# Turning the tokens of ten chunks with 32 by 32 block transposes on VectorE and a trip through DRAM, in place of TensorE transposes

## The chip, the core and the metric

The kernel runs on one core of a Trainium2 chip. The time is device time in microseconds (us) of one execution, the median of several runs. The engines are named as in the profile: PE is TensorE (PEld its weight loads), DVE is VectorE, ACT is ScalarE, POOL is GpSimd, SP is SyncE, which issues nearly all DMAs here.

## What is computed

Three layers follow each other, for batch 2, 768 tokens and 512 channels, all in float32. The part that the change touches is the middle one: each element of x is multiplied by the cosine and the sine of an angle, and the two products are mixed over the tokens.

```python
def _attn_ref(q, k, v):                      # 8 heads of 64: retention
    for t in range(S):
        state = gamma * state + outer(k[:, :, t], v[:, :, t])
        y[:, :, t] = scale * (q[:, :, t] @ state)

def _moe_ref(x, w_theta, w_tok_r, w_tok_i, w_ch):
    theta = x @ w_theta
    zr, zi = x * np.cos(theta), x * np.sin(theta)
    y = np.einsum('ts,bsd->btd', w_tok_r, zr) + np.einsum('ts,bsd->btd', w_tok_i, zi)
    u = x + y
    return u + np.maximum(u @ w_ch, 0.0)

def _moe2_ref(x, w_in, g_ln, w_sg, b_sg, w_out):
    h = gelu(x @ w_in); u, v = h[..., :512], h[..., 512:]
    v_s = np.einsum('ts,bsd->btd', w_sg, layernorm(v) * g_ln) + b_sg[None, :, None]
    return x + (u * v_s) @ w_out
```

## The kernel before

The 2 x 768 tokens are cut into twelve chunks of 128 tokens, 0 to 5 of the first batch and 6 to 11 of the second. A float32 product is made of three TensorE products of a high and a low part (`terms3`), so nearly every operand is split: ACT writes the high part (`split_hi`, L334), DVE the low part by a subtraction (`split_lo`, L340).

For each chunk, `retention` (L475) loads q, k and v in two halves of 512 KB (L460), forms scores (eight matmuls of 64 rows), a mask on DVE (L506), a faded v (ACT L529 or DVE L524), the outer products for the state, and `attend`. DVE then writes the chunk of x, L625, with the channels on the partitions and the tokens along the row (`x_chunk`), into the buffers `xa` and `xb`. `theta` (L647) multiplies it by the weights of the angle, in two halves of six matmuls of 512 columns, which gives angles with the tokens on the partitions; ACT and DVE make cosine and sine of them in one buffer `z` of 1024 words per partition. To be multiplied, x is needed with tokens on the partitions as well: `turn` (L717) has TensorE transpose four 128 by 128 blocks into a PSUM bank `tp`, and `times` (L725) is one DVE instruction of 1024 words that multiplies cosine and sine by it. z is split, and `mix_main` and `mix_rest` (L751, L778) mix it over tokens with weights that arrive as 1 MB loads (`weight`, L381: DMA, ACT L406, DVE L416 and L426, split). After them come the channel layer, the two up projections with gelu, the norm, the gate and the output products, none of which the change touches in what they compute.

An operation is an entry of a list of some 970. A table of numbers, `ORDER`, says in which order the planner (`Plan.schedule`) places them; it works out modelled start times with costs per engine, gives out buffers (`RAWS` raw loads, `PAIRS` buffers of 1024 words, `ONES` of 512) and sorts by start. Each engine then works through its own instructions in that order, and so does SP with the DMAs: a DMA that waits holds up those behind it. A gap of PE that the planner sees in the first microseconds is filled with idle matmuls on the identity (`keep_warm`).

Of the kernel before, what the change touches and what calls it, by code (L numbers as in the profile page):

```python
# [10 lines left out]
F32 = mybir.dt.float32  # L11
# [7 lines left out]
P = 128  # L19
# [17 lines left out]
N_WP = 19  # L37

RAWS, PAIRS, ONES = 2, 36, 7


class Buf:
# [21 lines left out]
class Plan:  # L64
# [105 lines left out]


ORDER = [
# [50 lines left out]
]  # L223


# [1 line left out]
def retention_spectral_gmlp(  # L227
# [10 lines left out]
):  # L238
    nc = tc.nc
    const = ctx.enter_context(tc.tile_pool(name="const", bufs=1))  # L240
    psum = ctx.enter_context(tc.tile_pool(name="psum", bufs=1, space=bass.MemoryType.PSUM))
    ctx.enter_context(tc.manual_schedule())
    V, A, G = nc.vector, nc.scalar, nc.gpsimd
# [19 lines left out]
    def bank():  # L263
        return Buf("psum")
# [33 lines left out]
    def x_chunk(i):  # L298
        b, c = divmod(i, NCH)
        if c < TA // P:  # L300
            return xa[b][:, :, c * P : (c + 1) * P]
        return xb[:, :, b, c * P - TA : (c + 1) * P - TA]
# [13 lines left out]
    def pe(dur, fn, **k):  # L316
        return plan.op("PE", dur, fn, **k)
# [5 lines left out]
    def dve(words, fn, ps=False, fast=False, **k):  # L323
        dur = 0.15 + words * (0.52e-3 if fast else 1.042e-3)
        return plan.op("DVE", dur, fn, port=not ps, **k)
# [149 lines left out]
    def retention(i):  # L475
# [168 lines left out]
            lambda: n4(h, F32R), lambda: n4(l, F32R), lambda: x_chunk(i), 512, t + 6, [*keys, h], [l]  # L644
        )

    def theta(i):  # L647
        b, c = divmod(i, NCH)
        t = T(i) + C['LT']
# [61 lines left out]
            w=[r],  # L711
            prio=t + 5.2,
        )
        tp = bank()
        keys = [("x", b, c, d) for d in range(NP)]

        def turn():  # L717
            for p in range(NP):
                nc.tensor.transpose(  # L719
                    out=ap(tp)[:, p * P : (p + 1) * P], in_=x_chunk(i)[:, p], identity=ident  # L720
                )

        pe(0.35, turn, form="turn", r=keys, w=[tp], prio=t + 5.3)

        def times():  # L725
            z2 = ap(z).rearrange("p (n t) -> p n t", n=2)
            V.tensor_tensor(  # L727
                out=z2, in0=ap(tp)[:, None, :].to_broadcast([P, 2, 512]), in1=z2, op=ALU.mult
            )

        dve(1024, times, ps=True, r=[tp], w=[co, r, z], prio=t + 6)
        split_hi(lambda: ap(zh, F32R), lambda: ap(z), 1024, t + 7, [z], w=[zh])
        split_lo(
            lambda: ap(zh, F32R), lambda: ap(zl, F32R), lambda: ap(z), 1024, t + 8, [z, zh], [zl]
        )
        zhl[i] = zh, zl

# [534 lines left out]
        weight(W_MAIN + s, T(s) + C['LW'])  # L1272
    for i in range(N):
        b, s = divmod(i, NCH)
        retention(i)
        theta(i)
        mix_main(b, s, T(i) + C['LM'])
        if i == NCH - 1:
            for k in range(NCH // 2):
                weight(W_REST + k, T(NCH) + C['LRW'] + 8 * k)  # L1280
        if s == NCH - 1:
            for k in range(NCH):
                mix_rest(b, k, T(i) + C['LR'] + (5 * k if b == 0 else 0.3 * k))
# [158 lines left out]
```

## Time and profile before

| | us |
|---|---|
| median of 3 runs (366.65 to 367.08) | 366.71 |
| the profiled execution | 367.32 |
| its span, first to last instruction | 365.6 |
| PE busy | 361.2 (99%) |
| DVE busy | 290.6 (79%) |
| ACT busy | 186.5 (51%) |
| POOL busy | 12.4 (3%) |

The span is what the trace shows; 1.72 us of the profiled execution lie around it. Busy times of engines overlap each other. A row of the timeline gives the start and the length of one merged run of instructions; the ends of matmuls are modelled, so for PE the distance between two starts is the better measure.

### The profile page before, as it was taken

To read this page: it belongs to the slowest core of one execution; us is meant where nothing else is said; L and a number is where in the kernel's file an instruction comes from. 1 tells how busy PE (TensorE), PEld (TensorE's weight loads), DVE (VectorE), ACT (ScalarE), POOL (GpSimd) and SP (SyncE) were. 2 spreads that over 40 slices of the span, in tenths; PEclk is the share of its full clock that TensorE was granted. 3 is DMA by queue.
4 is the path that set the end of the run, shared out by engine and by line. 5 is a ranking of instruction groups with operands and counts; after the bars stand their busy time and mean duration, and the time that the engine had idled before them with its cause. 6 is when DMAs were issued, how large, how long until landed. Compare 5 with 4: busy or idle time off the path is not lost.

```text
span 365.6 us, 5779 instructions
## 1 busy us (share of the span) xinstructions
PE 361.2 (99%) x2350; PEld 310.4 (85%) x2350; DVE 290.6 (79%) x456; ACT 186.5 (51%) x314; POOL 12.4 (3%) x18
## 2 busy tenths in 40 slices
PE   8999999999999999999999999999999999999996
PEld 7888888888999888888998888888888889988885
DVE  2788988987476978645688797989998996998894
ACT  3477979465363195611733434665687451252400
POOL 1021011000000220000000000000000000000000
PEclk9999999999999999999999999999999999999999
DMA  7999730174973411005042000001000000000034
GB/s 304 413 414 415 275 117 0 16 272 143 335 247 125 174 59 57 29 1 231 1 144 87 2 0 0 2 0 59 0 2 1 0 2 1 2 0 0 30 143 172
DMA packets 10346, 39.08 MB, mean 107 GB/s; under 512 B 1360, under 2 KB 2384, under 8 KB 7888
## 3 DMA queue, kind: packets, MB, share of 16 engines
q1 hardware_dynamic: 10176, 38.67, 28.3%
q8 instruction: 18, 0.29, 0.3%
q10 hardware_dynamic: 144, 0.05, 0.1%
q14 instruction: 8, 0.07, 0.1%
HBM read 35.57 MB, written 3.15 MB: 106 GB/s over the span
## 4 chain that ended last, share of the span: by engine, by line
PE 99%; DVE 0%; issue 0%
PE banks L314 97%; PE banks L719 1%; DVE b L1251 0%; DVE state L272 0%; DVE halfpi L276 0%
## 5 line engine op out<-in xcount | busy, mean ns | idle before, releaser
L314 PE MATMUL banks<-b,b 128*128 128x512 f32 (+2 forms) x1764 | 325.3, 351 | 0.0
L314 PEld LDWEIGHTS banks<-b,b 128*128 128x128 f32 (+1 forms) x1764 | 273.8, 183 | 45.6 <-issue 1.5
L334 ACT ACTIVATE b<-b 128x512 fp32r<-128x512 f32 (+1 forms) x83 | 62.6, 786 | 51.9 <-DVE b L1098 17.0
L340 DVE TENSOR_TENSOR b<-b,b 128x512 fp32r<-128x512 f32 (+1 forms) x83 | 70.2, 870 | 14.5 <-PE banks L314 8.9
L334 ACT ACTIVATE b<-xa 128x512 fp32r<-128x512 f32 (+1 forms) x26 | 17.0, 663 | 21.3 <-DVE xa L770 12.8
L406 ACT ACTIVATE b<-b 128x1024 f32<-128x1024 f32 x16 | 18.4, 1153 | 11.0 <-DMA b<-wts 11.0
L340 DVE TENSOR_TENSOR b<-xa,b 128x512 fp32r<-128x512 f32 (+1 forms) x26 | 18.7, 728 | 4.9 <-ACT b L334 4.9
L314 PE MATMUL banks<-b 64*128 64x128 f32 (+1 forms) x352 | 20.1, 262 | 0.0
L426 DVE SCALAR_TENSOR_TENSOR b<-b 128x1024 int32<-128x1024 int32 x16 | 19.5, 1220 | 0.5 <-ACT b L406 0.3
L314 PEld LDWEIGHTS banks<-b 64*128 64x128 f32 (+1 forms) x352 | 18.0, 171 | 1.9 <-issue 1.1
L506 DVE TENSOR_TENSOR b<-banks,causal 128x512 f32<-128x512 f32 x24 | 15.9, 685 | 4.5 <-PE banks L314 4.4
L334 ACT ACTIVATE b<-xb 128x512 fp32r<-128x512 f32 (+1 forms) x13 | 8.4, 669 | 18.9 <-DVE xb L806 6.3
L878 ACT ACTIVATE b<-b 128x512 f32<-128x512 f32 x24 | 14.8, 627 | 5.4 <-DVE b L868 5.4
L727 DVE TENSOR_TENSOR b<-banks,b 128x1024 f32<-128x1024 f32 x12 | 14.7, 1221 | 3.6 <-ACT b L710 1.4
L529 ACT ACTIVATE b<-b,dec 128x64 f32<-128x64 f32 x56 | 14.1, 334 | 5.4 <-DMA b<-qkv 5.4
L416 DVE TENSOR_SCALAR b<-b 128x1024 int32<-128x1024 int32 x16 | 10.9, 689 | 5.1 <-DMA b<-wts 5.1
L684 DVE SCALAR_TENSOR_TENSOR b<-banks,b 128x512 f32<-128x512 f32 x12 | 8.3, 689 | 7.9 <-PE banks L314 4.8
L675 ACT ACTIVATE b<-banks 128x512 int32<-128x512 f32 x12 | 7.1, 590 | 14.3 <-PE banks L314 14.3
L969 ACT ACTIVATE b<-b,rstd 128x512 f32<-128x512 f32 x12 | 9.6, 808 | 8.5 <-DVE rstd L958 8.5
L884 DVE SCALAR_TENSOR_TENSOR b<-b,banks 128x512 f32<-128x512 f32 x18 | 12.2, 680 | 1.7 <-ACT b L878 1.3
L868 DVE SCALAR_TENSOR_TENSOR b<-b,banks 128x512 f32<-128x512 f32 x18 | 11.9, 679 | 1.0 <-ACT b L860 0.9
L860 ACT ACTIVATE b<-banks 128x512 f32<-128x512 f32 x18 | 10.4, 593 | 4.5 <-PE banks L314 3.7
(74 smaller groups left out, 220.6 us busy)
## 6 DMA issues: line engine op xcount, KB each, us to landing
b<-wts SPq DMA_DIRECT2D x16, 1024.0 KB, 4.9
b<-qkv SPq DMA_DIRECT2D x24, 512.0 KB, 10.8
out<-b SPq DMA_DIRECT2D x11, 256.0 KB, 2.2
b<-wsg SPq DMA_DIRECT2D x9, 256.0 KB, 6.0
xa<-wts SPq DMA_DIRECT2D x2, 1024.0 KB, 11.7
xb<-wts SPq DMA_DIRECT2D x1, 1024.0 KB, 9.3
brow<-bvec SPq DMA_DIRECT2D x1, 384.0 KB, 5.8
dq<-qdecays SPq DMA_DIRECT2D x1, 256.0 KB, 6.3
```

The source lines that it names most:

```text
L314: nc.tensor.matmul(out=o, lhsT=l, rhs=r, start=start, stop=stop, skip_group_check=more)
L334: act(words, lambda: A.activation(out=hi(), in_=src(), func=AF.Copy), prio=prio, r=r, **k)
L340: lambda: E.tensor_tensor(out=lo(), in0=src(), in1=hi().bitcast(F32), op=ALU.subtract),
L406: lambda: A.activation(out=words(1).bitcast(F32), in_=words(1).bitcast(F32), func=AF.Prelu, scale=REBIAS, alpha=SIGN_UP,),
L416: lambda: V.tensor_scalar(out=words(0), in0=words(0), scalar1=29, scalar2=None, op0=ALU.logical_shift_right),
L426: lambda: V.scalar_tensor_tensor(out=words(0), in0=words(1), scalar=3, in1=words(0), op0=ALU.logical_shift_left, op1=ALU.bitwise_or,),
L506: V.tensor_tensor(out=ap(at[i])[:, h * 512 + lo : h * 512 + hi].rearrange("p (n t) -> p n t", n=n), in0=ap(sc[h])[:, lo:hi].rearrange("p ( ...
L529: A.activation(out=v, in_=v, func=AF.Copy, scale=dk[:, h : h + 1])
L727: V.tensor_tensor(out=z2, in0=ap(tp)[:, None, :].to_broadcast([P, 2, 512]), in1=z2, op=ALU.mult)
L868: lambda: V.scalar_tensor_tensor(out=ap(s), in0=ap(s), scalar=1.0 / GA, in1=ap(t), op0=ALU.add, op1=ALU.mult),
L878: lambda: A.activation(out=ap(s), in_=ap(s), func=AF.Tanh, scale=GA * GC),
L884: lambda: V.scalar_tensor_tensor(out=ap(o), in0=ap(s), scalar=1.0, in1=ap(t), op0=ALU.add, op1=ALU.mult),
```

## The change

Chunks 0 and 1 keep their `turn` on TensorE (`TURNED`). For the other ten, `by_token` takes the chunks in pairs (2 and 3, 4 and 5, 6 and 7, 8 and 9, 10 and 11). DVE transposes each chunk of x in blocks of 32 by 32 (`V.transpose`, 512 words per partition) into half of a buffer `tt`; SP writes `tt`, 512 KB, to a scratch tensor in DRAM; four DMAs of 128 KB read it back, each into 32 partitions, in runs of 256 words, so that the blocks land where a whole transpose would have put them. `times` becomes two DVE instructions of 512 words per chunk, which read the turned x from SBUF instead of a PSUM bank. The retention of a pair is listed before the angles of its first chunk, and the whole `ORDER` is another one. The counts of all other instructions stay, but for one `keep_warm` matmul less.

```diff
+TURNED = (0, 1)
...
 ORDER = [
-    48, 50, 49, 78, 77, 51, 105, 106, 0, 52, 161, 133, 55, 54, 56, 53, 189, 82, 57, 58, 134, 79, 6,
...
+    48, 50, 62, 49, 63, 105, 51, 106, 0, 52, 168, 118, 64, 53, 119, 55, 54, 56, 6, 67, 58, 57, 66,
...
+    dram = ctx.enter_context(tc.tile_pool(name="dram", bufs=1, space=bass.MemoryType.DRAM))
...
+    turned = {}
+
+    def by_token(i, t):
+
+        if i - i % 2 in turned:
+            return turned[i - i % 2]
+        tt, xt = Buf("pair"), Buf("pair")
+        turned[i - i % 2] = xt
+        for e in range(2):
+
+            def blocks(e=e):
+                V.transpose(
+                    out=ap(tt).rearrange("p (c e d k) -> p e d c k", c=4, e=2, d=NP)[:, e],
+                    in_=x_chunk(i + e).rearrange("p d (c k) -> p d c k", c=4),
+                )
+
+            b, c = divmod(i + e, NCH)
+            dve(
+                512, blocks, r=[("x", b, c, d) for d in range(NP)], w=[(tt, e)], prio=t + 4,
+            )
+        scr = dram.tile([P, 1024], F32, name=f"scr{i}")
+        dma(
+            512, lambda: nc.sync.dma_start(out=scr, in_=ap(tt)), r=[(tt, 0), (tt, 1)],
+            w=[("scr", i)], prio=t + 5,
+        )
+        for c in range(4):
+
+            def move(c=c):
+                nc.sync.dma_start(
+                    out=ap(xt)[32 * c : 32 * c + 32].rearrange("j (a q) -> j a q", a=4),
+                    in_=scr.rearrange("(a j) (c q) -> c j a q", a=4, c=4)[c],
+                )
+
+            dma(128, move, r=[("scr", i)], w=[(xt, c)], prio=t + 5)
+        return xt
...
+        if i in TURNED:
+            tp = bank()
...
+            dve(1024, times, ps=True, r=[tp], w=[co, r, z], prio=t + 6)
+        else:
+            xt = by_token(i, t)
+
+            def times(half):
+                v = ap(half).rearrange("p (d a k) -> p d a k", d=NP, a=4)
+                x = ap(xt).rearrange("p (a e d k) -> p e d a k", a=4, e=2, d=NP)[:, i % 2]
+                V.tensor_tensor(out=v, in0=x, in1=v, op=ALU.mult)
+
+            for half in (co, r):
+                dve(
+                    512, named(times, half), r=[(xt, a) for a in range(4)], w=[half, (z, half.k)],
+                    prio=t + 6,
+                )
...
-        retention(i)
+        if s % 2 == 0:
+            retention(i)
+            retention(i + 1)
         theta(i)
```

Three places where the order differs. The first is PE from its first matmul on. Before (`b_95`, `b_102`, `b_105`: q and k of chunks 0, 1, 2; `b_98`, `b_100`, `b_107`: their v; `ident` alone: keep-warm):

```order
L314 MATMUL banks<-state_64 128x128 x6
L314 MATMUL banks<-ident 128x128 x3
L314 MATMUL banks<-b_95 128x128 x8
L314 MATMUL banks<-ident 128x128 x2
L314 MATMUL banks<-b_98 64x64 x8
L314 MATMUL banks<-ident 128x128 x2
L314 MATMUL banks<-b_126,b_98 64x128 x8
L314 MATMUL banks<-b_102 128x128 x8
L314 MATMUL banks<-b_100 64x64 x8
```

After (`b_102`, `b_105`, `b_111`: q and k of chunks 0, 1, 2; `b_107`, `b_109`, `b_114`: their v):

```order
L319 MATMUL banks<-state_66 128x128 x6
L319 MATMUL banks<-ident 128x128 x3
L319 MATMUL banks<-b_102 128x128 x8
L319 MATMUL banks<-b_105 128x128 x8
L319 MATMUL banks<-ident 128x128 x3
L319 MATMUL banks<-b_107 64x64 x8
L319 MATMUL banks<-b_140,b_107 64x128 x8
L319 MATMUL banks<-b_111 128x128 x8
L319 MATMUL banks<-b_109 64x64 x8
L319 MATMUL banks<-b_105,state_67 64x128 x8
L319 MATMUL banks<-b_176,b_109 64x128 x8
L319 MATMUL banks<-b_114 64x64 x8
```

The scores of chunk 1 moved ahead of the first outer product, and the two gaps with two idle matmuls each became one gap with three.

The second place is SP's queue of DMAs after the first loads. Before (`xa`: the weights of the third mixing step; `b` from `wts`: later weights; `qkv`: later chunks):

```order
L395 DMA xa_87<-wts 128x2048
L460 DMA b_440<-qkv 128x1024
L395 DMA b_527<-wts 128x2048
L395 DMA b_628<-wts 128x2048
L395 DMA b_812<-wts 128x2048
L460 DMA b_820<-qkv 128x1024
```

After (`scr_91` and `scr_92`: the scratch of chunks 2 and 3, and of 4 and 5; `b_584`, `b_588`: chunk 9; `b_580`, `b_725`: the turned x of the two pairs):

```order
L400 DMA xa_89<-wts 128x2048
L674 DMA scr_91<-b_403 128x1024
L680 DMA b_580<-scr_91 32x4x256
L465 DMA b_584<-qkv 128x1024
L465 DMA b_588<-qkv 128x1024
L680 DMA b_580<-scr_91 32x4x256 x2
L400 DMA b_605<-wts 128x2048
L680 DMA b_580<-scr_91 32x4x256
L400 DMA b_675<-wts 128x2048
L674 DMA scr_92<-b_501 128x1024
L680 DMA b_725<-scr_92 32x4x256 x4
L400 DMA b_781<-wts 128x2048
```

The write and the four reads of a pair stand between loads of weights and of later chunks, and the last read of the first pair stands behind a 1 MB load.

The third place is DVE's queue where the first turned chunk is multiplied. Before (`L727`: `times` of chunk 1, from a PSUM bank):

```order
L340 TENSOR_TENSOR b_598<-b_367,b_586 128x1024
L570 TENSOR_TENSOR grown<-banks,state_65 128x256
L524 TENSOR_TENSOR b_379<-b_379,dec 128x2x256
L727 TENSOR_TENSOR b_475<-banks,b_475 128x1024
L340 TENSOR_TENSOR b_644<-b_463,b_632 128x1024
```

After (`L782`: `times` of chunk 2, from the turned x `b_580`; `L663`: the block transpose of chunk 5; the last row: the low part of z of chunk 2):

```order
L782 TENSOR_TENSOR b_614<-b_580,b_614 128x512
L663 STREAM_TRANSPOSE b_501<-xb 128x4x4x32
L431 SCALAR_TENSOR_TENSOR xa_89<-xa_89 128x1024
L529 TENSOR_TENSOR b_391<-b_391,dec 128x2x256
L782 TENSOR_TENSOR b_614<-b_580,b_614 128x512
L345 TENSOR_TENSOR b_715<-xa_89,b_706 128x1024
L511 TENSOR_TENSOR b_728<-banks,causal 128x512
L345 TENSOR_TENSOR b_731<-b_614,b_717 128x1024
```

One multiplication became two, with a block transpose and a weight's conversion between them, and they now wait for DMAs in place of PE.

## Rows read from the trace of the kernel before

**Rows 1.** The page, part 1: busy us, share of the span and instructions by engine.
```profile
PE 361.2 (99%) x2350; PEld 310.4 (85%) x2350; DVE 290.6 (79%) x456; ACT 186.5 (51%) x314; POOL 12.4 (3%) x18
```

**Rows 2.** The page, part 4: the chain that ended last, by engine and by line.
```profile
PE 99%; DVE 0%; issue 0%
PE banks L314 97%; PE banks L719 1%; DVE b L1251 0%; DVE state L272 0%; DVE halfpi L276 0%
```

**Rows 3.** Waits of PE: who for whom, us in total, times, longest.
```profile
PE banks L314 <- DVE halfpi L276: 1.2, 1, 1.2
```

**Rows 4.** Timeline of PE around turns (L719): start, length, line, operation, count.
```profile
54.24 0.60 PE L719 MATMUL banks<-ident,xa 128*128 128x128 f32 x4
54.59 1.63 PE L314 MATMUL banks<-b,b 128*128 128x512 f32 x6
56.06 0.60 PE L719 MATMUL banks<-ident,xb 128*128 128x128 f32 x4
56.41 8.44 PE L314 MATMUL banks<-b,b 128*128 128x512 f32 x36
64.69 0.60 PE L719 MATMUL banks<-ident,xa 128*128 128x128 f32 x4
...
133.72 16.59 PE L314 MATMUL banks<-b,b 128*128 128x512 f32 x72
150.15 0.60 PE L719 MATMUL banks<-ident,xb 128*128 128x128 f32 x4
```

**Rows 5.** Timeline of PE between retention matmuls and groups of 512 columns.
```profile
37.31 7.10 PE L314 MATMUL banks<-b,b 128*128 128x512 f32 x30
...
44.34 1.09 PE L314 MATMUL banks<-b,state 64*64 64x128 f32 x16
```

**Rows 6.** Timeline of PE at the start, to the first angles at 21.75.
```profile
5.37 2.08 PE L314 MATMUL banks<-b 64*128 64x128 f32 x16
...
7.38 0.71 PE L314 MATMUL banks<-ident 128*128 128x128 f32 x4
...
8.02 0.69 PE L314 MATMUL banks<-b 128*64 128x64 f32 x16
...
21.75 3.04 PE L314 MATMUL banks<-b,b 128*128 128x512 f32 x12
```

**Rows 7.** Timeline of ACT: the faded v of a chunk.
```profile
11.68 2.00 ACT L529 ACTIVATE b<-b,dec 128x64 f32<-128x64 f32 x8
```

**Rows 8.** DVE groups by form: busy us, mean ns of one, idle before.
```profile
L340 DVE TENSOR_TENSOR b<-b,b 128x512 fp32r<-128x512 f32 x55 | 36.1, 686 | 3.4 <-ACT b L334 3.2
L340 DVE TENSOR_TENSOR b<-b,b 128x1024 fp32r<-128x1024 f32 x28 | 34.3, 1233 | 11.1 <-PE banks L314 8.9 <-ACT b L334 2.1
...
L727 DVE TENSOR_TENSOR b<-banks,b 128x1024 f32<-128x1024 f32 x12 | 14.7, 1221 | 3.6 <-ACT b L710 1.4 <-ACT b L702 1.4 <-PE banks L719 0.8
...
L570 DVE TENSOR_TENSOR grown<-banks,state 128x256 f32<-128x256 f32 x8 | 3.3, 416 | 0.9 <-PE banks L314 0.9
```

**Rows 9.** Timeline of DVE: three instructions in a row, from start to start.
```profile
48.87 0.69 DVE L524 TENSOR_TENSOR b<-b,dec 128x512 f32<-128x512 f32 x1
49.47 1.23 DVE L727 TENSOR_TENSOR b<-banks,b 128x1024 f32<-128x1024 f32 x1
50.60 1.22 DVE L340 TENSOR_TENSOR b<-b,b 128x1024 fp32r<-128x1024 f32 x1
```

**Rows 10.** Stretches: us, busy PE, PEld, DVE, ACT, POOL, PEclk, DMA share, GB/s.
```profile
27.40:36.60 9.20, 9.20 (x106) 7.79 (x106) 7.92 (x12) 7.07 (x17) 1.70 (x2) 1.00 1.03 414
36.60:45.70 9.10, 9.10 (x66) 7.34 (x66) 8.32 (x12) 9.10 (x24) 0.00 (x0) 1.00 0.72 275
...
64.00:73.10 9.10, 9.10 (x45) 7.55 (x44) 8.32 (x10) 3.91 (x5) 0.00 (x0) 1.00 0.12 16
...
250.00:300.00 50.00, 50.00 (x228) 41.66 (x227) 45.34 (x114) 33.46 (x58) 0.00 (x0) 1.00 0.00 1
```

**Rows 11.** DMA issues: count, KB each, median us from issue to landing.
```profile
out<-b SPq DMA_DIRECT2D x2, 128.0 KB, 1.7
```

More of the change, by code (lines that the diff above doesn't have):

```diff
@@ L713, in theta, with turn, times @@
         )
[L714 to L720, printed above, removed]
-                )
[L723 to L732, printed above, removed]
+        if i in TURNED:
+            tp = bank()
+            def turn():
+                for p in range(NP):
+                    nc.tensor.transpose(
+                        out=ap(tp)[:, p * P : (p + 1) * P], in_=x_chunk(i)[:, p], identity=ident
+                    )
+            pe(
+                0.35, turn, form="turn", r=[("x", b, c, d) for d in range(NP)], w=[tp],
+                prio=t + 5.3,
+            )
+            def times():
+                z2 = ap(z).rearrange("p (n t) -> p n t", n=2)
+                V.tensor_tensor(
+                    out=z2, in0=ap(tp)[:, None, :].to_broadcast([P, 2, 512]), in1=z2, op=ALU.mult
+                )
+            dve(1024, times, ps=True, r=[tp], w=[co, r, z], prio=t + 6)
[9 more added lines that the diff above has]
+                    prio=t + 6,
+                )
+        split_hi(
+            lambda: ap(zh, F32R), lambda: ap(z), 1024, t + 7, [z, (z, 0), (z, 1)], w=[zh]
+        )
         split_lo(
-            lambda: ap(zh, F32R), lambda: ap(zl, F32R), lambda: ap(z), 1024, t + 8, [z, zh], [zl]
+            lambda: ap(zh, F32R), lambda: ap(zl, F32R), lambda: ap(z), 1024, t + 8,
+            [z, (z, 0), (z, 1), zh], [zl],
         )
```

100 rows, old and new, of the table ORDER are left out of this document.

## The prediction, made before the change was run

> **What bounds the kernel now.** I read the busy times first: PE is busy for 361.2 of 365.6 us, DVE for 79%, ACT for half [rows 1]. Then the chain that ended last, followed back from the end: it is PE for 99%, and 1% of it is the line of the turn itself [rows 2]. Then PE's waits: one, of 1.2 us, before its first matmul [rows 3]. So after the start PE waits for nobody; the time is the sum of what PE executes plus what its start loses. An instruction taken from PE is worth its whole length, as long as nothing that takes its place comes late. That is the question here: the ten turns leave PE, and DVE and the DMA queues get work that z, and so PE, depends on.
>
> **What goes, and what it is worth.** The timeline of PE shows turns alone between groups of six matmuls [rows 4]. From the start of a turn to the start of the group behind it: 54.59 - 54.24 = 0.35 us, the same at 56.06. Then the group behind a turn: 56.06 - 54.59 = 1.47. What is a group without a turn ahead? From 56.41 to 64.69 are six groups in 8.28, from 133.72 to 150.15 twelve in 16.43; the difference is six groups in 8.15, or 1.36 each. So a turn costs 0.35 and makes the group behind it 0.11 longer: 0.46. The change takes away ten of twelve: **4.6 us**. All of it lies on PE, and PE is the chain.
>
> **What the new order adds on PE.** Going from groups of 512 columns to retention's matmuls and back costs too: the five groups from 37.31 to 44.34 take 7.03 [rows 5], where five times 1.36 is 6.80, so a trip costs 0.23. Counting in the two orders, PE makes five such trips before and six after: +0.2. All other matmuls are the same in number and form. Net on PE: **-4.4**.
>
> **The start.** PE's first score begins at 5.37, the first angles at 21.75 [rows 6]. In between PE has two gaps filled with idle matmuls; one is the pair of two at 7.38, which takes 0.64 to the next start at 8.02. After, the scores of chunk 1 fill the first gap, and one gap of three remains, about 0.96. That would gain some 0.6. But the outer product of chunk 2 then comes earlier, at about 14.4 by adding the rows up, and it needs v of chunk 2 faded by ACT, which takes 2.0 [rows 7]. In the new order this stands behind the split of x of chunk 0, which itself comes later than before, since chunk 0's v is loaded third and not second; I get 12.9 + 2.0 = 14.9 and a wait of 0.5. I take the start at no gain, with 0.6 to either side.
>
> **What DVE gets.** A 512-word instruction lasts 0.686, a 1024-word one 1.22 [rows 8]; in a row they follow each other at 0.60 and 1.13 [rows 9]. Two multiplications of 512 words for one of 1024: 2 x 0.60 - 1.13 = +0.07. The block transpose isn't in this trace. Its nearest rows: an operation on 256 words at 0.416 is the floor, one on 1024 words at 1.233 the ceiling [rows 8]; I take 0.60, as any other pass over 512 words. It can't cost less than nothing, being added. So each chunk adds 0.67, ten of them 6.7, on an engine with 75 us of idle time in the span. The tight place is where DVE is densest, 27 to 73: 7.9 to 8.3 of 9.2 in each stretch [rows 10]. Four transposes and the multiplications of chunks 2 and 3 fall there, some 2.6 us in 46, which makes 88% into 94%. It still fits, with PE's needs as the measure (next part). At the ceiling the same stretch gets 2.5 more and is full.
>
> The Trainium skill, in "VectorE: DVE Perf Modes", section "The three transpose paths", gives VectorE 311 ns for a 128 by 128 block in bf16 and TensorE 390; four such blocks would be an estimate of 1.24 us per chunk on DVE, near the ceiling above. By the same figures a turn would be worth 1.56 on PE; the rows show 0.46, so I don't use its figures in the sum. No row shows a transpose on DVE.
>
> **What the trip through DRAM takes, and whether PE waits for it.** Take the first pair, chunks 2 and 3. Adding up PE's steps, the attend of chunk 3 ends at about 25, DVE's queue reaches the second transpose at about 32, and SP issues the write of 512 KB then. It joins a backlog: the 16 DMA engines run at 414 GB/s to 36.6 and at a mean of 275 over the next 9.1 us [rows 10], so at full rate the backlog lasts 6.0 us more, to 42.6. The bytes up to this write are the same in both orders, so it lands at about 42.6. The reads follow. A DMA of 128 KB in runs of 1 KB takes 1.7 from issue to landing when nothing is ahead [rows 11]; but between the first and the last read stand two loads of 512 KB and one of 1 MB, together with the reads 2.6 MB or 6.3 us: landed at 50.6. SP itself waits for the write to land, from 33 to 42.6, and what is queued behind it are chunk 9's q, k and v and a weight of the fifth mixing step, none needed before 60. DVE reaches the first multiplication by x of chunk 2 at about 53 by the same adding: it doesn't wait. From there to the low part of z are eight instructions, 6.6 us by rows 9, so z is whole at 59.6. PE needs it at about 62.8: before, mixing began 1.5 ahead of 54.24; after, two attends and an outer product fewer and two groups of angles more stand ahead of it (-0.8), and eight groups of chunks 0 and 1 follow (10.9). **Room: 3 us on DVE, 6 on the DMAs.** For chunk 3 the queue of DVE is held until about 66.5 by x of chunk 6, which waits for PE; five instructions later, at 71.3, its z is whole and PE comes at 73.0: room 1.7. For the last pair the final read stands behind a 1 MB load that waits for a raw buffer; I get z of chunk 10 at 148.4 and PE at 150.3: room 2. The pairs between have more. Cover for all of it is thus PE's own backlog of mixing groups; if it is gone, each us of lateness is a us of PE.
>
> **The sum.** Profiled execution before 367.32, span 365.6, 1.72 around it. Span after: 365.6 - 4.6 + 0.2 = 361.2; with 1.7 around it 362.9 for a profiled execution. The median of the runs is 0.61 below the profiled one, so **362.3**. The end is the same as before, two small products and their stores.
>
> **The rivals.**
> - *Some of it is given back as waits for DVE* (363.3 to 366.0). For it: DVE at 94% in 27 to 73; rooms of 1.7 to 3; from 250 to 300 DVE is busy 91% [rows 10], and that stage stands in another order too. Against it: before, PE had no wait at as dense a load [rows 3]. If transposes take the ceiling's 1.13 in a row instead of 0.60, the first pairs lose 2.1 of room, and two or three places lose 0.5 to 1.5: about 364.5.
> - *Slower: the strided reads are slow* (373 or more). Each read fills 32 partitions with runs of 1 KB from 128 places. If it runs at a tenth of the rate of a plain load, 3.2 us in place of 0.32, four reads are 11.5 late, and all behind them in SP's queue. DVE then stands still at the first multiplication, with a weight's conversion, a fade and a mask behind it, and PE waits 11.5 - 6 for chunk 2 and 11.5 - 2 for chunk 10: 15 us, 377. It decides from a lateness of about 6.7 (0.7 and 4.7 of waits are over the 4.4 + 0.7): reads at a sixth of the rate. Against it: a store of the same size and runs takes 1.7 in all [rows 11], of which a sixth of the rate would already fill 1.9.
> - *The gain is used up at the start or the rest by the new order* (366.0 to 367.4): the start would have to lose 0.6 and waits another 3 or more. The order of all other work is new as well, so this can't be ruled out.
> - *The transposes don't leave PE*: excluded, the order of PE has two turns left.
>
> The Trainium skill bears on the slow rival: the same page and section warn that a plain DMA that transposes by strides is 19 times slower than the hardware's transpose when the innermost stride at the destination is large. Here the blocks are turned on DVE and the innermost run is 256 words on both sides, so by its own condition the rule shouldn't bite; if it did, the reads would be slower than in the tenth above. No row shows a read from DRAM in such pieces.
>
> **How the numbers follow.** Forecast (361.4 to 363.3, the start's 0.6 either way and up to 0.4 of small waits): 0.62. Waits for DVE: 0.23. Gain used up: 0.05. Slow reads or another late hop, slower than before: 0.08. Faster still, below 361.4, if the start gains its 0.6 without the wait and the trips cost nothing: 0.02. A measurement of this kernel can tell 0.2%, 0.7 us, from no change: faster by over that 0.87, within 0.05, slower 0.08. The range takes in the forecast and most of the waits: 361.3 to 365.3.
>
> **What would show it.** PE's row of the turn: 8 instructions where there were 48, and no wait of PE after the start. DVE: ten rows of the transpose at about 0.69 each; 1.2 would speak for the first rival. The first multiplication with an idle time that ends on a DMA of `scr` would be the hop's lateness; a time from issue to landing of over 4 us for the reads where nothing else is queued would make it the second. First angles later than 22.3 would be the start. The forecast is wrong if PE's row of waits shows more than 1 us against DVE or a DMA, or if groups of 1.36 became longer.

## The result, and the profile after

| kernel | median us | executions | ratio to before, 95% interval |
|---|---|---|---|
| before | 366.68 | 366.15 to 367.08 (4) | |
| after | 362.83 | 362.75 to 362.92 (4) | 0.9896, 0.9879 to 0.9913 |

The change makes the kernel faster by 1.04%, 3.85 us; the prediction said 362.3 in a range of 361.3 to 365.3. The profiled execution of after takes 362.86, its span is 361.1. That span is 4.5 below that of before (365.6); why the medians differ by 0.6 less is told under "The sum".

The page of after, busy us by engine, against [rows 1]:

```profile
PE 356.1 (99%) x2308; PEld 305.0 (84%) x2308; DVE 295.5 (82%) x476; ACT 187.0 (52%) x314; POOL 9.0 (3%) x18
```

PE executes 5.1 us less, DVE 4.9 more, and PE is still what is busy all the time. The waits of PE (for whom, us in total, times, longest), against [rows 3]:

```profile
PE banks L319 <- DVE halfpi L281: 1.2, 1, 1.2
PE banks L319 <- DVE b L345: 0.5, 1, 0.5
```

One wait is new, and it belongs to the start. The chain that ended last, in order of time (start, length, what), against [rows 2]:

```profile
4.77 10.56 DMA xb<-wts
15.33 0.02 issue
15.36 1.22 ACT xb L411
16.58 0.02 issue
16.60 1.24 DVE xb L431
17.84 0.02 issue
17.86 1.18 ACT b L339
19.04 0.02 issue
19.06 1.24 DVE b L345
20.30 0.04 issue
20.34 18.55 PE banks L319 x226
38.89 0.59 PE banks L760 x4
39.48 318.51 PE banks L319 x1840
```

From 20.34 on it is PE without a break, as before. Ahead of that stands now the first angle weight: it lands at 15.33, and four passes turn it into its high and low parts. PE had begun its first angles at 19.08 and stands until the low part is there. The new instructions on DVE (busy us, mean ns of one | idle before), against [rows 8]:

```profile
L782 DVE TENSOR_TENSOR b<-b,b 128x512 f32<-128x512 f32 x20 | 13.2, 680 | 0.1
...
L663 DVE STREAM_TRANSPOSE b<-xa 128x512 f32<-128x512 f32 x6 | 4.2, 702 | 0.0
...
L663 DVE STREAM_TRANSPOSE b<-xb 128x512 f32<-128x512 f32 x4 | 2.8, 704 | 0.0
```

Ten transposes of 0.70 us, and almost no idle time ahead of the multiplications: in this trace they don't stand still for the trip through DRAM. Its DMAs (count, KB each, median us from issue to landing):

```profile
scr<-b SPq DMA_DIRECT2D x5, 512.0 KB, 4.6
b<-scr SPq DMA_DIRECT2D x20, 128.0 KB, 3.1
```

### The profile page after: what moved, and what is told of

It is laid out like the page before. It is cut to its first block, busy times and chain, and to the rows that moved or that the text cites. A ratio compares the mean times of both kernels' runs of the same rounds, so it can differ in the third digit from the quotient of the medians.

```text
span 361.1 us, 5762 instructions
## 1 busy us (share of the span) xinstructions
PE 356.1 (99%) x2308; PEld 305.0 (84%) x2308; DVE 295.5 (82%) x476; ACT 187.0 (52%) x314; POOL 9.0 (3%) x18
## 4 chain that ended last, share of the span: by engine, by line
PE 93%; DMA 4%; DVE 1%; ACT 1%; issue 0%
PE banks L319 93%; DMA xb<-wts 3%; DMA dec<-decays 1%; DVE xb L431 0%; DVE b L345 0%; ACT xb L411 0%; ACT b L339 0%; PE banks L760 0%; DVE b L1311 0%
## 5 line engine op out<-in xcount | busy, mean ns | idle before, releaser
L339 ACT ACTIVATE b<-b 128x512 fp32r<-128x512 f32 (+1 forms) x83 | 63.4, 788 | 72.0 <-PE banks L319 26.4
L920 ACT ACTIVATE b<-banks 128x512 f32<-128x512 f32 x18 | 10.2, 589 | 9.3 <-PE banks L319 9.1
L782 DVE TENSOR_TENSOR b<-b,b 128x512 f32<-128x512 f32 x20 | 13.2, 680 | 0.1
L1202 ACT ACTIVATE b<-banks 128x512 f32<-128x512 f32 x8 | 4.7, 593 | 14.2 <-PE banks L319 13.0
```

The source lines that it names most:

```text
L339: act(words, lambda: A.activation(out=hi(), in_=src(), func=AF.Copy), prio=prio, r=r, **k)
L782: V.tensor_tensor(out=v, in0=x, in1=v, op=ALU.mult)
```

## What a turn is worth, in both directions

Theory: 0.35 us of its own and 0.11 on the group behind, whichever kernel it stands in. In the kernel before, ten turns are not executed; in the kernel after, ten are executed again.

```diff
# the kernel before
         def turn():
-            for p in range(NP):
+            for p in range(NP if i < 2 else 0):
# the kernel after
             def angle(half=half):
+                if half == 0 and i not in TURNED:
+                    for p in range(NP):
+                        nc.tensor.transpose(out=ap(th)[:, p * P : (p + 1) * P], ...)
```

> The kernel before, with the turns of chunks 2 to 11 not executed (40 of PE's 48 transposing matmuls left out); the multiplications of those chunks read whatever the bank holds, all else is as before. It asks what a turn is worth on PE. Theory: a turn costs its 0.35 us and makes the group behind it 0.11 longer, so ten are 4.6: 366.7 - 4.6 = 362.1 (361.9 to 362.4), and PE has no wait after its start. Rival one: only the 0.35 are won, since the group behind is longer for another reason: 366.7 - 3.5 = 363.2. Rival two: PE runs into DVE: 364.5 or more, with a wait of PE against DVE of over 1 us in sum.

Measured: 362.43, ratio 0.9887 (0.9872 to 0.9902). By medians that is 3.9 under before in the same comparison (366.34) and 4.3 under the median that the prediction read (366.71), between theory and the rival. The traces decide: compared start by start, PE's lead over the traced execution of before grows by 0.35 to 0.37 at a turn and by 0.08 to 0.12 at the group behind it, at all ten places. The span falls by 4.5 (365.6 to 361.1); 0.4 of this comes from the first scores, and 0.3 is lost again in a wait at 121, so the turns are 4.5 in sum. The rival of 3.5 falls.

> The kernel after, with the ten turns executed on PE again as well: ahead of the first group of angles of chunks 2 to 11, into the bank that the angles then overwrite; nothing uses them, and the block transposes and the trip through DRAM stay. It asks the price of a turn in the new order. Theory: 362.8 + 10 x 0.46 = 367.4 (367.1 to 367.7), slower than before by the little that the new order costs on PE without the turns. Rival one: 0.35 each, 366.3. Rival two: the new kernel has slack on PE that the trace does not show, so less than half of it comes: under 365.2.

Measured: 367.65, ratio 1.0031 (1.0020 to 1.0041); 4.8 more than after, by medians and by spans. Each added turn delays PE by 0.44 to 0.47. Timeline of PE of this kernel around one of them:

```profile
30.79 3.02 PE L319 MATMUL banks<-b,b 128*128 128x512 f32 x12
33.64 0.60 PE L698 MATMUL banks<-ident,xa 128*128 128x128 f32 x4
33.99 2.33 PE L319 MATMUL banks<-b,b 128*128 128x512 f32 x9
```

From the turn's start to the next group it is 0.35 again. It follows that the gain is the turns, and that the rest of the change gives nothing: with them put back, the new kernel is slower than before by 0.2 to 0.4%.

## What the trip through DRAM costs

```diff
-        tt, xt = Buf("pair"), Buf("pair")
+        tt = xt = Buf("pair")
 ...
-            512, lambda: nc.sync.dma_start(out=scr, in_=ap(tt)), ...
+            512, lambda: None, ...
             def move(c=c):
-                nc.sync.dma_start(out=ap(xt)..., in_=scr...)
+                pass
```

> The kernel after, without the trip through DRAM: the five writes of 512 KB and the twenty reads of 128 KB are left out, and the multiplications read the block-transposed tile itself (so their rows stand at the wrong tokens); the ten transposes stay on DVE. It asks what the trip costs. Theory: nothing, it lies beside PE's backlog: 362.8 (362.5 to 363.0). Rival: it costs something by its traffic, by SP's 45 us of waiting or by late products: 362.2 or less.

Measured: 362.95, ratio 0.9900 (0.9886 to 0.9914), against 362.83 for after. In both traces z of each chunk is whole at the same time within 0.1 (chunk 2: 60.56 and 60.63; chunk 10: 148.59 and 148.62). The trip is free as it stands, and DVE's queue, not the trip, says when z is whole. But it is only just free: at the last pair the last read lands at 143.89, and DVE comes to the multiplication at 143.97.

Then the reads are made more expensive, in two steps: four of 32 KB in place of each of 128 KB, and those also in runs of 128 bytes.

```diff
+                for a in range(4):
+                    nc.sync.dma_start(
-                    out=ap(xt)[32 * c : 32 * c + 32].rearrange("j (a q) -> j a q", a=4),
-                    in_=scr.rearrange("(a j) (c q) -> c j a q", a=4, c=4)[c],
+                        out=ap(xt)[32 * c : 32 * c + 32, 256 * a : 256 * a + 256],
+                        in_=scr[32 * a : 32 * a + 32, 256 * c : 256 * c + 256],
 and for the second step, with the multiplication reading the blocks in that order:
+                        out=ap(xt)[32 * c : 32 * c + 32].rearrange("j (m a k) -> a j m k", m=8, a=4)[a],
+                        in_=scr.rearrange("(a j) (c m k) -> a c j m k", a=4, c=4, m=8)[a, c],
```

> The kernel after, with each read of 128 KB made as four of 32 KB, still in runs of 1 KB: 16 reads for a pair, not 4, each about 0.45 us of SP. It is the control for the run below, and delays the last read by up to 12 x 0.45 = 5.4 us. Theory: the first multiplications then wait for the reads; of the delay DVE had nothing to spare at the last pair (multiplication at 143.97, read landed at 143.89) and about 1.6 at the first (53.98 against 52.40), and z had 1.9 and 2.3 of room ahead of PE: PE waits 0 to 2 at each of them, 363.0 to 366. Rival (the trip is wholly free at any length): 362.8.

Measured: 369.23 (368.30 to 370.20), ratio 1.0072 (1.0045 to 1.0098): slower than before, and more than either theory gave. The waits of PE in this kernel:

```profile
PE banks L319 <- DMA b<-qkv: 2.7, 1, 2.7
PE banks L319 <- DVE b L345: 1.5, 2, 1.3
```

The longest is not for the tokens at all but for a load of q and k. It is that of chunk 10. In after it is issued at 98.36 and lands at 105.60, 2.4 ahead of its scores. Here it stands in SP's queue behind the third pair's sixteen reads, issued 0.46 apart where nothing holds them up, is itself issued at 105.01 and lands at 111.53. What follows is seen in stretches of this kernel (us, busy PE, PEld, DVE, ACT, POOL, then PE's granted clock, DMA share, GB/s):

```profile
105.00:108.90 3.90, 3.87 (x72) 3.42 (x70) 2.54 (x5) 2.30 (x5) 0.00 (x0) 1.00 0.92 311
108.90:111.60 2.70, 0.03 (x2) 0.03 (x2) 0.39 (x1) 1.94 (x3) 0.00 (x0) 1.00 1.04 429
111.60:113.00 1.40, 1.40 (x18) 1.28 (x19) 0.24 (x1) 0.00 (x0) 0.00 (x0) 0.98 0.94 392
113.00:115.00 2.00, 2.00 (x12) 2.00 (x11) 2.00 (x4) 0.96 (x1) 0.00 (x0) 0.50 0.57 225
115.00:117.00 2.00, 2.00 (x8) 1.67 (x8) 1.88 (x4) 0.24 (x1) 0.00 (x0) 0.66 0.61 242
117.00:119.00 2.00, 2.00 (x18) 1.95 (x17) 0.69 (x1) 0.33 (x1) 0.62 (x1) 1.00 0.00 0
```

PE stands for 2.7 us, works on at 1.00, and is then granted 0.50, the lower of its two levels (1.2 and 2.4 GHz), for some 3 us; that costs 1.5 more. So one late load cost 4.3 us in this execution. The mean granted clock was 0.995 here and in the one of 370.20, and 0.999 in those of 368.30 and 368.60: there the fall must be missing.

The reads themselves come late too, and DVE stands still for them at the multiplications of chunks 2, 8 and 10:

```profile
DVE b L783 <- DMA b<-scr: 6.6, 3, 3.0
```

The 3.0 are at chunk 8. Behind them in DVE's queue is the low part of x of chunk 10, and the wait of 1.3 above is PE's for that. My expectation had counted the lateness of the reads at each z, and not what is queued behind them, in SP's queue or in DVE's.

> The kernel after, with the same 16 reads of 32 KB for a pair, but in runs of 128 bytes (the tile holds the blocks in another order, which the multiplication reads back): eight times as many pieces. It asks whether the forecast's slow rival would have come with short runs. Theory (time goes by the piece below 1 KB): a pair's reads hold the 16 DMA engines not 1.3 but up to 10 us, z of the first and last pair is late by 5 or more over the run above, DVE stands and PE with it: 370 to 400. Rival (time goes by bytes): as the run above within 0.5.

Measured: 374.18 (370.47 to 375.12), ratio 1.0193 (1.0139 to 1.0247). The time lies in the range of "time goes by the piece", but not for its reason. The reads by themselves hardly notice the short runs: the sixteen of the second pair, with nothing else queued, take a mean of 2.24 us from issue to landing against 1.79 in runs of 1 KB, and over the kernel the packets of SP's queue take 34.3% of the 16 engines' span against 32.8%. The DMA row (median us to landing) of this kernel:

```profile
b<-scr SPq DMA_DIRECT2D x80, 32.0 KB, 2.5
```

And that of the kernel with sixteen reads in runs of 1 KB:

```profile
b<-scr SPq DMA_DIRECT2D x80, 32.0 KB, 1.9
```

So "time goes by the piece", eight times as much, falls, and "as the run above within 0.5" falls as well: the 5 us over the run above are real. In the two traces it is 5.3. The greater part are the same waits grown longer: the one for chunk 10's q and k is 4.7 here, the one for the low part of x 1.9, and there is a new one of 1.0 for z of chunk 2. Another 1.6 is a second stretch at the lower clock, behind the wait of 1.9 (columns as above):

```profile
114.50:117.92 3.42, 3.13 (x21) 2.90 (x22) 1.02 (x2) 0.77 (x2) 0.00 (x0) 0.50 0.45 182
141.81:145.22 3.41, 3.41 (x9) 2.65 (x9) 3.41 (x5) 1.31 (x3) 0.00 (x0) 0.50 0.98 327
```

A kernel whose loads already come late pays for every further delay in SP's queue.

## Where DVE's room ends

Each block transpose is done two, three and four times.

```diff
             def blocks(e=e):
-                V.transpose(out=ap(tt)..., in_=x_chunk(i + e)...)
+                for _ in range(2):    # then 3, then 4
+                    V.transpose(out=ap(tt)..., in_=x_chunk(i + e)...)
```

> The kernel after, with each of the ten block transposes done twice, one behind the other: 10 x 0.6 to 0.7 more on DVE, 6 to 7 us. It asks how much room DVE has. Theory: the first pair had 3 us of room, the second chunk of it 1.7, the last pair 2, and each pair comes 1.2 to 1.4 later: all is covered, 362.8 to 363.3, waits of PE against DVE after the start below 0.5. Rival (DVE is as good as the bound, the forecast's rival of waits): the first pairs come late by what is added, 2 or 3 places of 0.5 to 1.5, 364.0 to 366.0.

Measured: 362.85, ratio 0.9898 (0.9884 to 0.9912); no change. The room at z of chunks 2, 5, 9 and 10 shrinks by 0.9 to 1.2, to 1.1, 1.2, 1.6 and 0.9, and nothing is late.

> The kernel after, with each of the ten block transposes done four times in a row: 3 x 0.62 = 1.9 us more of DVE for each chunk, 19 in all. It asks where DVE's room ends. In the trace of after z is whole ahead of PE's need by 2.3 us (chunk 2), 1.6 (3), 3.1 (4), 2.0 (5), 2.6 (9), 1.9 (10); with the transposes twice these were 1.1, 1.5, 3.0, 1.2, 1.6 and 0.9, so some 1.1 less at four of them. Theory (room is counted at each z, and DVE's queue sets when z is whole): two more passes take 2.2 more, so chunks 2, 5, 9 and 10 come late by 0.5 to 1.3; a lateness of PE moves the later needs too, so 0.9 to 3 us in sum: 363.8 to 366, with waits of PE against DVE behind 60 us. Rival (room is DVE's idle share of 18%, 65 us of which 19 are taken): nothing shows, 362.7 to 363.2.

Measured: 373.81, ratio 1.0202 (1.0187 to 1.0217): 11.0 over after. Both lines are far off. So a run between the two was needed, with a new theory beside the two old ones.

> The kernel after, with each block transpose done three times in a row: 12.4 us more on DVE in all, between twice (no change) and four times (11 us slower). It asks what decides where DVE's room ends. Theory one, the idle time of the dense stretch: from 27.4 to 73.1 DVE is busy 42.3 of 45.7 us in after and 44.8 with the transposes twice; a third pass makes 47.3, 1.6 over; and z of chunks 9 and 10 keep 0.6 and nothing, so 364.4 to 366.0, with waits of PE against DVE from 30 us on. Theory two, only the room at each z counts: z of chunk 2 just in time, 362.8 to 363.4. Theory three, a straight line from twice to four times: 368.3.

Measured: 366.47, ratio 0.9993 (0.9984 to 1.0003): 3.6 over after. Theory one, the idle time of the dense stretch, is the nearest, with a price some 0.5 too low; the room at z alone and the straight line both fall. The stretch from 27.4 to 73.1 (columns as above) in the trace of after:

```profile
27.40:73.10 45.70, 45.70 (x393) 38.02 (x390) 42.34 (x56) 36.12 (x66) 1.23 (x2) 1.00 0.69 255
```

With the transposes twice:

```profile
27.40:73.10 45.70, 45.70 (x393) 38.02 (x392) 44.81 (x60) 35.17 (x65) 1.23 (x2) 1.00 0.71 255
```

Three times:

```profile
27.40:73.10 45.70, 44.79 (x382) 35.88 (x379) 44.63 (x60) 33.58 (x63) 1.23 (x2) 1.00 0.65 235
```

Four times:

```profile
27.40:73.10 45.70, 42.40 (x342) 33.35 (x340) 44.51 (x60) 31.91 (x60) 1.23 (x2) 1.00 0.60 219
```

DVE (the third pair of numbers) goes from 42.3 to 44.8 and then no further: no run here gets more than 98% into this stretch. One more pass over the four transposes in it is 2.5 us. The second pass just fits. The third makes PE 2.6 late by 73 us (start left out), the fourth 5.5. The fourfold kernel's waits of PE show why the room at z was the wrong measure:

```profile
PE banks L319 <- DVE b L345: 5.5, 9, 1.3
PE banks L319 <- DVE b L726: 1.4, 2, 1.0
```

Nine waits for low parts, of which one is that of the start, and two for a bank that DVE has yet to free (L726). The first of the new ones ends at 32 us and is for the low part of a weight; a bank follows at 44, x of a chunk at 48, and z of chunk 2 only at 67.7. DVE works through its queue in order, so a full queue makes everything in it late. The waits cost more than their rows say: the new ones for DVE are 6.4 us in sum, where 11.0 are lost. One of 0.71 at 139.6 puts PE back by 0.98 from start to start.

## The start, and a version that is faster than both

The passes over the first angle weight are cut into halves, so that each follows the one ahead of it by half a weight.

```diff
+        parts = [slice(0, 512), slice(512, 1024)] if k == W_THETA else [slice(0, 1024)]
 ...
-            lambda: A.activation(out=words(1)..., in_=words(1)..., func=AF.Prelu, ...),
+            lambda: [A.activation(out=words(1)[:, s]..., in_=words(1)[:, s]..., ...) for s in parts],
 (likewise the pass on DVE, the high part on ACT and the low part on DVE)
```

> The kernel after, with the conversion of the first angle weight (two passes on ACT, two on DVE, each over 1024 words) cut into halves of 512 words, so that each pass follows the one before it by a half. Nothing is left out. In the trace of after PE waits inside its first group of angles for the low part of this weight (group of 2.29 where 1.46 is usual), and the chain that ended last runs from this weight's load through the four passes, 15.33 to 20.30. Theory: that wait is 0.8 us of the time; the low part is whole by about 18.7 and PE's chain moves to the front: 362.0 (361.8 to 362.3), with the DMA and the weight's passes gone from the chain. Rival: the next arrival takes the wait's place (x of chunk 0, a load, or z of chunks 2, 3 and 10 with their 1.6 to 2.3 of room): 362.5 or more.

Measured: 362.34, ratio 0.9889 (0.9875 to 0.9904), between theory and rival. In its trace the wait is gone and the chain is PE alone:

```profile
PE 99%; DVE 0%; issue 0%
```

But the 0.8 us that the first group of angles won was partly spent: the first scores ran slower than in the trace of after and put the first angles 0.56 later. So it was run again beside after on one chip.

> The kernel after, unchanged, as the measure for the two runs below on the same chip. All theories: 362.8 (362.7 to 363.0). What is looked at besides is the spread: kernel before's executions lie between 366.2 and 367.3, those of after within 0.2. Theory: PE's first matmuls come to their full pace at another time in each execution (5.0 to 7.8 us in the traces so far), and in after the wait for the angle weight hides it; then these executions stay within 0.3 of each other whenever the pace rises. Rival: the spread belongs to the chip, and after spreads as before does, by about 1 us.

> The kernel after with the first angle weight converted in halves, once more, beside after on the same chip. Theory: without the wait the time follows PE's first matmuls: 362.1 where they come early to full pace, 362.6 where late, median 0.5 under after (0.2 to 0.8), and a wider spread than after's. Rival: no gain on the same chip, within 0.2 of after.

Measured: after 362.93 (362.85 to 363.12), in halves 362.28 (362.13 to 362.40), ratio to before 0.9874 (0.9858 to 0.9889). The gain is 0.65 and its executions don't overlap with those of after: this version is the fastest here. After spreads by 0.3, before in the same comparison by 1.1 (366.19 to 367.31), as theory had it. The halved kernel does not spread wider than after in this run (0.3), as it had in the one above (0.5); that part of the expectation didn't come. How the first scores differ is seen in PE's count of matmuls from 5.40 to 6.40 (columns as above; the granted clock of these three rows is explained below them). In before:

```profile
5.40:6.40 1.00, 1.00 (x11) 1.00 (x11) 0.59 (x1) 0.00 (x0) 0.00 (x0) 1.00 1.01 414
```

In after:

```profile
5.40:6.40 1.00, 1.00 (x22) 1.00 (x22) 0.00 (x0) 0.00 (x0) 0.00 (x0) 1.00 1.05 430
```

In after without the trip through DRAM:

```profile
5.40:6.40 1.00, 1.00 (x11) 1.00 (x12) 0.00 (x0) 0.00 (x0) 0.00 (x0) 1.00 1.01 418
```

After has 22 matmuls where before and the kernel without DRAM have 11, and yet the last two have spans of 361.1 and 361.2: in after, PE waits for the weight anyhow.

The 1.00 in these rows is no reading. The trace of before has its first record of the granted clock at 7.31, that of the kernel without DRAM at 6.81, and the trace of after has none; where there is no record the table counts 1.00. In the thirteen traces that have one, it is a record of 1.00 and stands between 4.22 and 7.44, and PE's pace doubles at that place, within 0.3 us. Before it, the sixteen matmuls of a chunk's scores take as long as they do under a recorded 0.50, as the scores of chunk 10 are in the kernel with runs of 128 bytes:

```profile
114.79 2.08 PE L319 MATMUL banks<-b 64*128 64x128 f32 x16 [4.72 <-DMA b<-qkv]
```

In before the same sixteen take 2.08 from 5.37; in after thirty-two take 2.06 from 5.15. So the first scores run as they do at the lower level of the clock until the first record of 1.00, and that comes at another time in each execution.

> The kernel before, unchanged, for a second trace of it. Its executions spread over 1.1 us (366.2 to 367.3, spans 364.4 to 365.6); the one that the prediction read has a span of 365.6 and 11 matmuls of PE between 5.40 and 6.40 us, where traces with an early rise of PE's pace have 22. Theory: before's time follows the pace of the first scores, since nothing waits behind them: if this trace has about 22 there, its span is 364.4 to 364.8 and the first angles start about 1 us before 21.75; if it has 11, the span is 365.2 to 365.6. Rival: the spread comes from elsewhere, and the span does not go with that count.

Measured: 11 matmuls again, a span of 365.4, and all of the 0.2 that it lies under the first trace is gained ahead of 7.9 us, in the first scores; the first record of the clock stands at 6.99, 0.32 earlier. That agrees, but it is the late case a second time; no trace of before with an early rise was caught, so that this makes the whole spread of before is likely, not shown.

## Why the prediction was right, point by point

- **What bounds**: held. PE has no wait behind 20.34, and its last matmul starts at 357.70 where it was 362.11, 4.4 earlier; the prediction's net on PE was 4.4.
- **Turns, 4.6**: held; 4.5 taken out of before, 4.7 put back into after.
- **Trips, +0.2**: not seen by itself. With the ten turns put back the span is 0.4 above that of before (366.0 and 365.6), where trips and start together were to make 0.2.
- **Start, no gain, 0.6 to either side**: right in sum, wrong in place, so in part by luck: another wait of the same size stood in for the one that I had looked for. The first scores begin 0.2 earlier and two gaps with idle matmuls have become one, but the first group of angles lasts 2.29 where 1.46 to 1.50 is usual. The wait that I had looked for, 0.5 at the outer product of chunk 2, is not there; that step failed in adding up ACT's queue: ACT begins the fade at 11.74, not at 12.9. I hadn't followed the angle weight, whose load lands 1.3 later (13.99 to 15.33), although seven loads stand ahead of it in SP's queue in both kernels, six halves of q, k and v and one of decays. The DMA packets of the two traces suggest why. In after a packet of 16 KB, of the queue that the page lists as instruction, starts at 12.10 and takes 1.11; all but three of the weight's 128 packets have started by 13.35, and those three start at 13.96, 14.27 and 14.58. In before that packet starts at 13.97, and the weight's last at 13.15. In all eleven traces of the new order it starts ahead of the weight's last packet, in all three of the old order behind it, but no run moved it by itself: this cause is likely, not shown.
- **DVE**: a transpose measured 0.70 against 0.69, in a row 0.63 against 0.60; the second pass over ten of them 6.3. The sum of busy time grew by 4.9, not by 6.7. The lengths of DVE's instructions grew by 8.0 in sum, the transposes and the multiplications, but an instruction that follows another at once begins before the other's end, and that overlap grew by 3.0 (24.4 to 27.5): I had allowed for it at the new instructions alone. In 27 to 73 it went from 88.8% to 92.6%, where the prediction had 94%. The Trainium skill, in "VectorE: DVE Perf Modes", section "The three transpose paths", gives 311 ns for a 128 by 128 block in bf16; the estimate of 1.24 us for four of them is not what these rows show, 0.70 in float32.
- **DRAM trip**: held closely. Last read of the first pair 52.40 (50.6 predicted), first multiplication 53.98 (53). z of chunks 2, 3 and 10 whole at 60.56, 71.58, 148.59 (59.6, 71.3, 148.4), PE there at 62.66, 72.95, 150.28 (62.8, 73.0, 150.3).
- **The sum**: the predicted profiled execution was 362.9 with a span of 361.2; it measured 362.86 and 361.1. What was off by 0.5 is the last step, the median taken 0.61 below the profiled execution as in before. After's median lies 0.03 below, since its executions hardly spread. For the same reason the medians differ by 3.85 and not by the 4.5 of the spans: the profiled execution of before is 0.6 longer than its median, and that of after is not.
- **Rival, waits for DVE**: didn't come, and its price at the ceiling (364.5) was too high: the doubled transposes, a pair of which takes 1.4 from start to the next instruction, are dearer than that case (1.13), and cost nothing. From there on it was too low.
- **Rival, slow reads**: didn't come. Reads with little ahead take 2.5 to 3.1 us, from issue to landing. The same section of the Trainium skill warns that a plain DMA which transposes by strides is 19 times slower than the hardware's transpose when the innermost stride at the destination is large; no run here has such a stride. Runs of 128 bytes made a read of 32 KB 0.45 us slower. Where the reads were made later, with sixteen for a pair, the way that I had named came, DVE standing still at the multiplications (6.6 us in sum), and it held PE up for a small part of the loss; the larger part, 4.3, came by a way that I hadn't named, SP's queue and a load of q and k behind the reads.

## What to carry to other kernels

Where one engine is the whole chain, an instruction moved off it is worth its distance from start to start plus what it does to its neighbour, and the price on the other side is nothing up to a point: here that point was near the idle time of the densest stretch of the engine that takes the work, not its share over the span. Count what a new DMA puts ahead of others in its queue before counting how long it takes. A wait at the start can hide a spread that the kernel before shows, so carry a profiled execution over to a median only with the spread of the kernel that is meant.

## What was not expected of the hardware

- PE's first scores run at half the number of matmuls in one execution and at the full number in another (11 and 22 in the same us): the first record of a granted clock of 1.00 stands at 4.22 us in one trace and at 7.44 in another, and the pace doubles there.
- After standing for 2.7 us PE went on at a granted clock of 1.00 to 0.98 for 1.4 us and only then fell to 0.50, for some 3 us; the wait of 2.7 cost 4.3.
- A second pass over the ten transposes, 6.3 us of DVE, cost nothing, the third 3.6 us, the fourth 7.3.
